# Products pre-added from five chunks to two instead of three, in a ring of four buffers

## The chip, the cores and the metric

The kernel runs on one core of one Trainium2 chip. The metric is the device time of one execution in microseconds (us); lower is better. Profiles come from the hardware profiler, one execution each.

## The reference

The input x has S = 2048 tokens of D = 640 numbers in bf16. It is layer-normalised, and the result xn feeds two branches whose outputs are added to x:

```python
xn = layernorm(x)                                  # no scale, no bias
# A: sliding, dilated attention; H = 32 heads of 20, W = 8 positions, step 2
q, k, v = split(xn @ wqkv)
logits[s, w] = (q[s] . k[s - 2*w]) * 20**-0.5      # -1e9 where s - 2*w < 0
o[s] = sum_w softmax(logits[s])[w] * v[s - 2*w]
A = o @ wo
# B: bilinear gated linear unit, F = 1536
B = ((xn @ w_gate) * (xn @ w_up)) @ w_down
out = x + A + B
```

## The kernel before

Everything stays in on-chip memory after loading. The 640 channels lie as NCH = 5 chunks of 128 partitions, tokens along the free dimension. The tokens are handled in two halves of HS = 1024 for the logits, in eight blocks of SB = 256 for the attention sums, in four blocks of 512 for gate and up, and in 16 tiles of 128 for the output.

*Stages on TensorE (PE).* Projections of q and k (L437, L444 for the first half, L424 for the second) and of v (L424); logits (L485); gate and up (`glu`, L577), each group five matmuls of 128x512; and the output tile (`tail`, L608): 12 matmuls with the weights WD of the down projection, then five with WO on the attention result VO. A tile takes two tails, one for each half of its 640 columns.

*Logits.* For each half there are four pairs of window positions (`pair`, `qk_steps`). VectorE (DVE) multiplies q by shifted k for both positions of a pair and all five chunks (L467). Instead of handing five chunks of products to PE it keeps the first NKC = 3 in a buffer SL, puts the other two in TMP, and adds these onto two of the kept ones (L475). PE then sums over channels with a matrix of ones, G: NKC chunks times four quarters of the tokens, 12 matmuls of 32 output rows a pair. The four quarters lie in four column groups of the array. Two pairs make one batch; `qk_logits` issues its 24 matmuls, and ScalarE (ACT) copies the result to LOG (L492).

*Softmax and attention.* `softmax_steps` has a head on DVE (maximum, L501; subtraction, L516), the exponential on ACT, and a rest on DVE (sums, reciprocal, product L525). `attn_move` copies the weights to the four channel rows of each head by 16 DMAs into ATB. `pv_steps(b)` makes the attention sum of block b: one product of 10240 elements into PVB (L551), then three adds (L546) of 5120, 2560 and 1280 elements, the last of which writes the block into VO. Tiles 2b and 2b + 1 read it in their WO matmuls.

*Other DVE work.* The multiplication of gate by up (L582), and the evacuation of each tail with the residual XR (L612).

*Memory.* SL is a ring of NSL = 3 buffers. WD and WO are later loaded to the same place, so `down_loads` and `out_loads` wait for the logits matmuls of the buffers that they overwrite. PVB lies on the last ring buffer and TMP.

*Order.* A Python planner writes the program out before it is built. It counts the estimated time of PE and DVE (`t_pe`, `t_dve`), walks through DVE's steps in a fixed order, and after each step lets `run_fill` issue PE work from a list up to DVE's time. A batch of logits gets a due time 0.3 us after its products, and is put into PE's order when `t_pe` has come to it. Down tails may be issued only when their block is:

```python
if it[0] == "dn":
    if pv_done[0] <= it[1] or not loaded:
        return
```

Gate and up for the token blocks 0 and 1 stand in the list ahead of the tails of block 0. Whatever a list item does on DVE (a multiplication, an evacuation) takes its place in DVE's order at the moment when the item is issued. Every engine then works in the order written, and semaphores hold back an instruction until what it needs is there.

Of the kernel before, what the change touches and what calls it, by code (L numbers as in the profile page):

```python
# [5 lines left out]
FP16 = mybir.dt.float16  # L6
ACT = mybir.ActivationFunctionType
ALU = mybir.AluOpType
# [3 lines left out]
NCH = 5  # L12
# [4 lines left out]
W = 8  # L17
# [11 lines left out]
HS = S // 2  # L29
SB = 256  # L30
# [11 lines left out]
class Sched:  # L42
# [50 lines left out]
    def op(self, eng, fn, r=(), w=(), dma=False, name="", group=None):  # L93
        X = _Op()
        X.eng, X.fn, X.name, X.dma = eng, fn, name, dma
        X.needs_tick, X.event, X.pre_know, X.idx = False, None, None, len(self.ops)
        rk = [k for a in r for k in self.keys(a)]
        wk = [k for a in w for k in self.keys(a)]
        deps = {}
        inorder = eng in ("pe", "act", "dve")  # L100
        for k in rk:
            st = self.state.get(k)
            if st is not None:
                for o in st[0]:
                    deps[o.idx] = o
        for k in wk:
            st = self.state.get(k)
            if st is None:
                continue
            if group is not None and st[2] == group and not st[1]:  # L110
                for o in st[3]:
                    deps[o.idx] = o
                continue
            for o in st[0]:
                if not (eng == "pe" and o.eng == "pe"):
                    deps[o.idx] = o
            for q in st[1]:
                if eng in ("pe", "act") and q.eng == eng and not q.dma:
                    continue
                deps[q.idx] = q  # L120
        last = {}
        keep = []
        for d in deps.values():
            if d.dma or d.eng == "pool":
                keep.append(d)
            else:
                b = last.get(d.eng)
                if b is None or b.idx < d.idx:
                    last[d.eng] = d
        X.deps = keep + list(last.values())  # L130
        for d in X.deps:
            if not d.dma:
                d.needs_tick = True
        for k in rk:
            st = self.state.get(k)
            if st is None:
                self.state[k] = [[], [X], None, []]
            elif inorder and st[1] and st[1][-1].eng == eng and not st[1][-1].dma:
                st[1][-1] = X
            else:  # L140
                st[1].append(X)
        for k in wk:
            st = self.state.get(k)
            if group is not None and st is not None and st[2] == group and not st[1]:
                st[0].append(X)
            else:
                before = [] if st is None else st[0] + st[1]
                self.state[k] = [[X], [], group, before]
        if dma:
            X.event = (self.nc.alloc_semaphore(f"dma{self.n_dma}"), 16)  # L150
            self.n_dma += 1
        self.ops.append(X)
        return X
# [59 lines left out]
def build_kernel(nc, A_x, A_wqkv, A_wo, B_x, B_w_gate, B_w_up, B_w_down, out):  # L213
    K = Sched(nc)
    op = K.op

    place = [16512]

    def sb(name, shape, dtype=BF16, at=None):
        n = mybir.dt.size(dtype)  # L220
        for s in shape[1:]:
            n *= s
        n = (n + 63) // 64 * 64
        if at is None:
            at = place[0]
            place[0] += n
        assert at + n <= 229344, (name, at + n)
        return K.sbuf(name, shape, dtype, at)
# [1 line left out]
    WG = sb("WG", [128, NCH, F])  # L230
    WU = sb("WU", [128, NCH, F])
    a_pr = place[0]
    NKC = 3
    NSL = 3
    WD = sb("WD", [128, NF, D], at=a_pr)
    WO = sb("WO", [128, NCH, D], at=a_pr + NF * D * 2)
    SL = [sb(f"SL{s}", [128, 2, NKC, HS], FP16) for s in range(NSL)]
    PVB = sb("PVB", [128, NCH, W, SB], FP16, at=place[0] - 2 * NKC * HS * 2)
    TMP = sb("TMP", [128, 2, NCH - NKC, HS], FP16)
    XNT = sb("XNT", [128, NCH, S])  # L240
    VO = sb("VO", [128, NCH, VP + S])
# [40 lines left out]
    def dma(o, i, r=(), w=(), name="", eng="sp", group=None):  # L282
# [8 lines left out]
       r=[IDENT[:]], w=[IDENT[:]], name="ident")  # L291
# [3 lines left out]
       r=[G[:]], w=[G[:]], name="g1")  # L295
    op("pool", lambda e: e.affine_select(G[:], G[:], pattern=[[-4, H]], compare_op=ALU.is_ge,
                                         fill=0.0, base=0, channel_multiplier=1),
       r=[G[:]], w=[G[:]], name="g2")
# [109 lines left out]
    def bank():  # L408
        b = bank_ring.pop(0)
        bank_ring.append(b)  # L410
        return b
# [46 lines left out]
    def qk_steps(h, p, s):  # L458
        kept, tmp = SL[s], TMP
        kp = KH[h][:, 0, 0:1].ap[0]  # L460

        def prod(o, c0, c1):
            q = QH[h][:, c0:c1, :]
            k = KH[h][:, c0:c1, 4 * p:4 * p + HS + 2]
            kw = bass.AP(k.tensor, k.offset, [kp, [2, 2], [KL, c1 - c0], [1, HS]])
            qw = q.unsqueeze(1).to_broadcast([128, 2, c1 - c0, HS])
            return lambda: op("dve", lambda e: e.tensor_tensor(o[:], qw, kw, ALU.mult), r=[q, k], w=[o[:]],  # L467
                              name=f"prod{h}_{p}_{c0}")

        a, b = kept[:, :, 0:NCH - NKC, :], tmp[:]  # L470
        return [
            (0.16 + 2 * NKC * HS / 1920, prod(kept, 0, NKC)),
            (0.16 + 2 * (NCH - NKC) * HS / 1920, prod(tmp, NKC, NCH)),
            (0.16 + 2 * (NCH - NKC) * HS / 1920,
             lambda: op("dve", lambda e: e.tensor_tensor(a, a, b, ALU.add), r=[a, b], w=[a], name=f"psum{h}_{p}")),  # L475
        ]

    def qk_logits(h, batch):
# [57 lines left out]
    def pv_steps(b):  # L536
# [8 lines left out]
        def add(o, x, y, name):  # L545
            return lambda: op("dve", lambda e: e.tensor_tensor(o, x, y, ALU.add), r=[x, y], w=[o], name=f"{name}_{b}")  # L546

        P4, P2 = PVB[:, :, 0:4], PVB[:, :, 0:2]
        return [
            (0.16 + NCH * W * SB / 1920,  # L550
             lambda: op("dve", lambda e: e.tensor_tensor(PVB[:], vw, aw, ALU.mult), r=[v, a], w=[PVB[:]], name=f"pv_{b}")),  # L551
            (0.16 + NCH * 4 * SB / 1920, add(P4, P4, PVB[:, :, 4:8], "pa4")),
            (0.16 + NCH * 2 * SB / 1920, add(P2, P2, PVB[:, :, 2:4], "pa2")),
            (0.16 + NCH * SB / 1920, add(o, PVB[:, :, 0], PVB[:, :, 1], "pa1")),
        ]
# [104 lines left out]
    for t0 in (0, 2):  # L660
# [3 lines left out]
        for which in (0, 1):  # L664
            for t in (t0, t0 + 1):
                b = bank()
# [16 lines left out]
    for t0 in (4, 6):  # L683
        for g in range(5):
            b = bank()
# [85 lines left out]
    def step(it):  # L771
        it[1]()
        t_dve[0] += it[0]
        run_fill(t_dve[0])

    slot = [0]

    def pair(h, p):
        s = slot[0] % NSL
        slot[0] += 1  # L780
        assert all(s != x for _, ps, _ in batches for _, x in ps)
        for it in qk_steps(h, p, s):
            step(it)
        return p, s
# [4 lines left out]
    def settle():  # L789
        while batches:  # L790
            run_fill(batches[0][2] + 0.01)
        t_dve[0] = max(t_dve[0], t_pe[0] + 1.6)

    batch(0, [pair(0, 0), pair(0, 1)])
    batch(0, [pair(0, 2), pair(0, 3)])
    headA, restA = softmax_steps(0)
    force_fill(QKB)
    t_dve[0] = max(t_dve[0], t_pe[0] + 0.8)
    b0 = pair(1, 0)
    settle()  # L800
    for it in headA:
# [34 lines left out]
def bass_parallel_sum__sliding_local_dilated__glu_gated_bilinear__prompt_kernel(  # L836
    nc, A_x, A_wqkv, A_wo, B_x, B_w_gate, B_w_up, B_w_down, out
):
    build_kernel(nc, A_x, A_wqkv, A_wo, B_x, B_w_gate, B_w_up, B_w_down, out)
# [28 lines left out]
```

## Time and profile before

| what | us |
|---|---|
| median of three runs | 262.35 (261.96 to 262.42) |
| the profiled execution | 262.42 |
| its span, first to last instruction | 260.7 |
| PE busy | 255.6 |
| DVE busy | 216.1 |
| ACT busy | 107.3 |

| DVE instruction | elements | count | ns each |
|---|---|---|---|
| L467 product into SL | 6144 | 8 | 3352 |
| L467 product into TMP | 4096 | 8 | 2302 |
| L475 add | 4096 | 8 | 2290 |
| L551 attention product | 10240 | 8 | 5488 |
| L546 attention adds | 5120, 2560, 1280 | 8 of each | 2817, 1484, 819 |
| L582 gate times up | 512 | 48 | 417 |
| L612 evacuation | 320 | 31 | 487 |

Successive instructions of an engine can overlap by some tens of ns, and a matmul's duration holds its way through the array, so start times tell more than durations where many follow each other. Idle time that is given with an arrow (`<-PE PS L608`) ended when that instruction did. In the chain, each piece is followed back to what released it.

### The profile page before, as it was taken

To read this page: it belongs to the slowest core of one execution; us is meant where nothing else is said; L and a number is where in the kernel's file an instruction comes from. 1 tells how busy PE (TensorE), PEld (TensorE's weight loads), DVE (VectorE), ACT (ScalarE), POOL (GpSimd) and SP (SyncE) were. 2 spreads that over 40 slices of the span, in tenths; PEclk is the share of its full clock that TensorE was granted. 3 is DMA by queue.
4 is the path that set the end of the run, shared out by engine and by line. 5 is a ranking of instruction groups with operands and counts; after the bars stand their busy time and mean duration, and the time that the engine had idled before them with its cause. 6 is when DMAs were issued, how large, how long until landed. Compare 5 with 4: busy or idle time off the path is not lost.

```text
span 260.7 us, 4018 instructions
## 1 busy us (share of the span) xinstructions
PE 255.6 (98%) x1669; PEld 150.7 (58%) x1669; DVE 216.1 (83%) x240; ACT 107.3 (41%) x193; POOL 6.7 (3%) x13
## 2 busy tenths in 40 slices
PE   7999999899999999999999999999999999999996
PEld 3899855354554444444467744446774444777775
DVE  5799889999999999998847999999999999422221
ACT  3565558555657555565630035551004555000000
POOL 2000050000200000000000000000000000000000
DMA  6968889400000275065001376000311000021301
GB/s 202 326 136 148 100 226 402 156 3 0 0 3 0 50 206 144 0 208 219 3 0 57 97 199 175 0 4 0 99 54 50 0 3 0 27 74 53 101 28 50
DMA packets 21922, 23.46 MB, mean 90 GB/s; under 512 B 9872, under 2 KB 19472, under 8 KB 21904
## 3 DMA queue, kind: packets, MB, share of 16 engines
q1 hardware_dynamic: 21760, 23.04, 31.2%
q8 instruction: 13, 0.21, 0.3%
q10 hardware_dynamic: 144, 0.16, 0.2%
q14 instruction: 5, 0.04, 0.0%
HBM read 14.42 MB, written 2.62 MB: 65 GB/s over the span
## 4 chain that ended last, share of the span: by engine, by line
PE 80%; DVE 14%; SPq 2%; DMA 2%; ACT 1%; issue 1%
PE PS L577 40%; PE PS L608 28%; PE PS L424 10%; DVE SL L467 3%; SPq L283 2%; DVE XNS L371 2%; PE PS L485 2%; DVE STATS L354 2%; DVE SL L475 2%; DVE TMP L467 2%; DVE STATS L348 2%; DMA XST<-in_A_x_dram 2%; DVE MV L360 1%; DVE SD L369 1%; ACT KH L451 0%
## 5 line engine op out<-in xcount | busy, mean ns | idle before, releaser
L577 PE MATMUL PS<-XNT,WG 128*128 128x512 bf16 x240 | 59.6, 379 | 0.0
L577 PE MATMUL PS<-XNT,WU 128*128 128x512 bf16 x240 | 59.6, 379 | 0.0
L608 PE MATMUL PS<-WD,HT 128*128 128x320 bf16 (+1 forms) x396 | 57.6, 295 | 0.0
L579 ACT ACTIVATE HT<-PS 128x512 bf16<-128x512 f32 x48 | 28.7, 598 | 58.2 <-PE PS L577 58.2
L608 PEld LDWEIGHTS PS<-WD,HT 128*128 128x128 bf16 x396 | 38.1, 98 | 14.7
L551 DVE TENSOR_TENSOR PVB<-VO,ATB 128x10240 f16<-128x10240 bf16 x8 | 43.9, 5488 | 0.1
L424 PE MATMUL PS<-XNT,WQKV 128*128 128x512 bf16 x200 | 43.9, 379 | 0.0
L612 DVE TENSOR_TENSOR FOUT<-PS,XR 128x320 bf16<-128x320 f32 (+1 forms) x33 | 15.5, 477 | 30.4 <-PE PS L608 30.1
L577 PEld LDWEIGHTS PS<-XNT,WU 128*128 128x128 bf16 x240 | 23.4, 98 | 28.5 <-issue 0.4
L577 PEld LDWEIGHTS PS<-XNT,WG 128*128 128x128 bf16 x240 | 23.4, 98 | 28.2 <-issue 0.4
L579 ACT ACTIVATE USX<-PS 128x512 bf16<-128x512 f32 x48 | 28.7, 597 | 22.2 <-PE PS L577 20.8
L424 PEld LDWEIGHTS PS<-XNT,WQKV 128*128 128x128 bf16 x200 | 23.3, 118 | 20.2 <-issue 0.8
L546 DVE TENSOR_TENSOR PVB<-PVB 128x5120 f16<-128x5120 f16 (+1 forms) x16 | 34.4, 2150 | 0.0
L467 DVE TENSOR_TENSOR SL<-QH,KH 128x6144 f16<-128x6144 bf16 x8 | 26.8, 3352 | 1.4 <-ACT KH L451 1.4
L608 PE MATMUL PS<-WO,VO 128*128 128x320 bf16 (+1 forms) x165 | 27.1, 295 | 0.0
L582 DVE TENSOR_TENSOR HT<-HT,USX 128x512 bf16<-128x512 bf16 x48 | 18.5, 417 | 4.2 <-ACT USX L579 4.2
L608 PEld LDWEIGHTS PS<-WO,VO 128*128 128x128 bf16 x165 | 15.9, 98 | 5.9
L475 DVE TENSOR_TENSOR SL<-SL,TMP 128x4096 f16<-128x4096 f16 x8 | 18.3, 2290 | 0.2
L467 DVE TENSOR_TENSOR TMP<-QH,KH 128x4096 f16<-128x4096 bf16 x8 | 18.4, 2302 | 0.0
L430 ACT ACTIVATE VO<-PS 128x512 bf16<-128x512 f32 x20 | 11.9, 597 | 9.8 <-PE PS L424 9.8
L437 PE MATMUL PS<-XNT,WQKV 128*128 128x128 bf16 x200 | 12.6, 220 | 0.2
L437 PEld LDWEIGHTS PS<-XNT,WQKV 128*128 128x128 bf16 x200 | 11.6, 118 | 1.2 <-DVE XNT L394 0.5
(49 smaller groups left out, 137.8 us busy)
## 6 DMA issues: line engine op xcount, KB each, us to landing
ATB<-LOG SPq DMA_DIRECT2D x32, 128.0 KB, 2.6
XR<-in_A_x_dram SPq DMA_DIRECT2D x16, 160.0 KB, 2.3
XST<-in_A_x_dram SPq DMA_DIRECT2D x15, 160.0 KB, 3.9
out_dram<-FOUT SPq DMA_DIRECT2D x15, 160.0 KB, 1.8
WG<-in_B_w_gate_dram SPq DMA_DIRECT2D x1, 1920.0 KB, 9.5
WU<-in_B_w_up_dram SPq DMA_DIRECT2D x1, 1920.0 KB, 13.8
WD<-in_B_w_down_dram SPq DMA_DIRECT2D x1, 1920.0 KB, 8.2
WQKV<-in_A_wqkv_dram SPq DMA_DIRECT2D x10, 160.0 KB, 3.8
```

Source lines behind the costliest of these rows:

```text
L424: op("pe", (lambda l, x, c: lambda e: e.matmul(PS[:, b, :], l, x, start=(c == 0), stop=(c == NCH - 1)))(l, x, c), r=[l, x], w=[PS[:, b, :] ...
L430: op("act", lambda e: e.activation(o, PS[:, b, :], ACT.Copy), r=[PS[:, b, :]], w=[o], name=f"pev{which}_{m}_{j}")
L437: op("pe", (lambda o, l, x, st, sp: lambda e: e.matmul(o, l, x, start=st, stop=sp))(o, l, x, st, sp), r=[l, x], w=[o], name=f"pp{which}_{m ...
L467: return lambda: op("dve", lambda e: e.tensor_tensor(o[:], qw, kw, ALU.mult), r=[q, k], w=[o[:]], name=f"prod{h}_{p}_{c0}")
L475: lambda: op("dve", lambda e: e.tensor_tensor(a, a, b, ALU.add), r=[a, b], w=[a], name=f"psum{h}_{p}")),
L546: return lambda: op("dve", lambda e: e.tensor_tensor(o, x, y, ALU.add), r=[x, y], w=[o], name=f"{name}_{b}")
L551: lambda: op("dve", lambda e: e.tensor_tensor(PVB[:], vw, aw, ALU.mult), r=[v, a], w=[PVB[:]], name=f"pv_{b}")),
L577: op("pe", (lambda l, x, c: lambda e: e.matmul(PS[:, b, :], l, x, start=(c == 0), stop=(c == NCH - 1)))(l, x, c), r=[l, x], w=[PS[:, b, :] ...
L579: op("act", lambda e: e.activation(o, PS[:, b, :], ACT.Copy), r=[PS[:, b, :]], w=[o], name=f"guev{which}_{m}_{j}")
L582: h_pending.append(lambda: op("dve", lambda e: e.tensor_tensor(h, h, o, ALU.mult), r=[h, o], w=[h], name=f"h{m}_{j}"))
L608: op("pe", (lambda l, x, i, b: lambda e: e.matmul(PS[:, b, 0:wid], l, x, start=(i == 0), stop=(i == n - 1)))(l, x, i, b), r=[l, x], w=[PS[ ...
L612: op("dve", (lambda o, xr, b: lambda e: e.tensor_tensor(o, PS[:, b, 0:wid], xr, ALU.add))(o, xr, b), r=[PS[:, b, :], xr], w=[o], name=f"fi ...
```

## The change

Two chunks of products are kept instead of three. The three others go to TMP; two of them are added onto the two kept ones, and then the last is added onto the first kept one. So there are two adds for each pair in place of one, and eight logits matmuls in place of twelve. SL becomes a ring of four smaller buffers, which is entered at the last one, and PVB is put on the last ring buffer and the larger TMP as before. The total memory is the same.

```diff
-    NKC = 3
-    NSL = 3
+    NKC = 2
+    NSL = 4
...
-    PVB = sb("PVB", [128, NCH, W, SB], FP16, at=place[0] - 2 * NKC * HS * 2)
+    PVB = sb("PVB", [128, NCH, W, SB], FP16, at=place[0] + 4 * (NCH - NKC) * HS - 2 * NCH * W * SB)
...
-        a, b = kept[:, :, 0:NCH - NKC, :], tmp[:]
+        def add(a, b):
+            return lambda: op("dve", lambda e: e.tensor_tensor(a, a, b, ALU.add), r=[a, b], w=[a], name=f"psum{h}_{p}")
+
         return [
             (0.16 + 2 * NKC * HS / 1920, prod(kept, 0, NKC)),
             (0.16 + 2 * (NCH - NKC) * HS / 1920, prod(tmp, NKC, NCH)),
-            (0.16 + 2 * (NCH - NKC) * HS / 1920,
-             lambda: op("dve", lambda e: e.tensor_tensor(a, a, b, ALU.add), r=[a, b], w=[a], name=f"psum{h}_{p}")),
+            (0.16 + 4 * HS / 1920, add(kept[:, :, 0:2, :], tmp[:, :, 0:2, :])),
+            (0.16 + 2 * HS / 1920, add(kept[:, :, 0, :], tmp[:, :, 2, :])),
         ]
...
-        s = slot[0] % NSL
+        s = (slot[0] + NSL - 1) % NSL
```

The numbers ahead of the steps are the planner's times for them in us; with them, and with the shorter batches (0.2175 us for each pair and chunk), the planner writes another order. From L467 on, the line numbers of the changed kernel are up to two higher.

## The prediction

> **What bounds the kernel now.** I read the page first, for which engine is never idle.
>
> ```profile
> PE 255.6 (98%) x1669; PEld 150.7 (58%) x1669; DVE 216.1 (83%) x240; ACT 107.3 (41%) x193; POOL 6.7 (3%) x13
> PE   7999999899999999999999999999999999999996
> DVE  5799889999999999998847999999999999422221
> PE 80%; DVE 14%; SPq 2%; DMA 2%; ACT 1%; issue 1%
> ```
>
> TensorE (PE) is busy throughout and carries 80% of the chain of waits. But VectorE (DVE) is just as full, at 9 tenths, up to five sixths of the span: its 83% is an average over a full part and an empty end. A change that sends work from PE to DVE sends it to an engine with almost no room before 222 us. So I read the chain in order of time next, for where PE last waited for DVE.
>
> ```profile
> 49.35 0.83 PE PS L485 x12
> 50.18 14.16 PE PS L424 x65
> 64.34 1.44 PE PS L485 x24
> ...
> 110.59 1.41 PE PS L485 x24
> 112.00 20.61 PE PS L577 x95
> 132.61 18.47 PE PS L608 x136
> ```
>
> L485 are the logits matmuls (two pairs to a batch), L577 gate and up, L608 the output tiles ("tails"). From 50 us PE never stops. Note the 20.6 us of gate/up work between the last logits batch and the first tail. The third view is DVE's timeline under the first tails.
>
> ```profile
> 122.92 5.48 DVE L551 TENSOR_TENSOR PVB<-VO,ATB 128x10240 f16<-128x10240 bf16 x1
> ...
> 139.98 1.48 DVE L546 TENSOR_TENSOR PVB<-PVB 128x2560 f16<-128x2560 f16 x1
> 141.88 0.49 DVE L612 TENSOR_TENSOR FOUT<-PS,XR 128x320 bf16<-128x320 f32 x1 [0.42 <-PE PS L608]
> 142.29 0.81 DVE L546 TENSOR_TENSOR VO<-PVB 128x1280 bf16<-128x1280 f16 x1
> ```
>
> The L546 add at 142.29 completes attention block 1 at 143.10. The tail of token tile 2 needs it after four tails and its own 12 WD matmuls: 132.61 + 4 x 2.31 + 1.63 = 143.48. The margin is 0.4 us, and it exists because the big product of block 1 (L551, 122.92) ran before the tails began. The bracket shows the danger: DVE works in program order, and an evacuation (L612) makes it stand until PE has finished that tail.
>
> **PE saves 1.9 us.** Per pair 12 logits matmuls become 8, 32 fewer in all. A batch of 24 took 1.41 us, 0.0588 each: 32 x 0.0588 = 1.88 us.
>
> **DVE pays 10 us.** The two products keep their sizes, 6144 and 4096 elements, in the other order, and the 4096 add stays; a 2048 add comes on top, which reads what the 4096 add wrote. L546 gives its price: 2.82 us for 5120 elements and 1.48 for 2560 are 0.52 ns an element and 0.15 fixed, so 1.22 us, of which 0.08 overlap the next start; waiting for its predecessor costs 0.11 more. That is 1.25 us a pair, 10.0 in all, and a pair goes from 7.81 to 9.06. The first four pairs (33.56 us on) run back to back.
>
> Batch 1 now sits behind 95 L424 matmuls instead of 80. PE reaches it at 47.61 + 3.24 = 50.85, waits for the second pair (33.56 + 18.12 + 0.1 = 51.8) and leaves at 52.3. Batch 2 comes 75 matmuls later, 68.6; its second pair ends at 69.9, so PE waits 0.9 and leaves at 70.45. At the same amount of work the old kernel stood at 71.2: 0.7 gained. Batches 3 and 4: on DVE follow pair 5 (69.8 to 78.9), the maximum and subtraction (72.69 to 75.34 before, 2.65), pair 6 with six gate/up multiplications at 0.34 (between the adds they also hide the 0.11 and 0.11 of waiting: 8.84 + 2.04, to 92.4), the sum and division (83.47 to 88.19 before, 4.7, to 97.1), pairs 7 and 8 with five and six multiplications (10.5 and 10.9, to 118.5). PE adds up to 70.45 + 6.6 (30 L424) + 19.4 (90 L577) = 96.5 for batch 3, then 0.94 and 26.0 to 123.4 for batch 4: DVE is 4 and 5 us ahead, no wait, another 0.94 saved. PE is then ready for the first tail at 130.94 instead of 132.61. The ring of four and the moved slots add no wait here: each slot's last reader is a batch or more back.
>
> **What the slower pairs move: two things on the path.** The schedule is written from estimated times, so a later DVE puts logits batches later in PE's order. Comparing the two programs' instruction orders, only 30 gate/up matmuls (6.5 us) stand between batch 4 and the first tail, where 95 (20.6 us) stood.
>
> First, WD and WO are loaded into the slots that batch 4 reads. The SP queue issued WD 1.3 us into batch 4, landing took 8.2 us, WO's 9.7. Now WD goes out near 123.75 and lands at 131.95, WO goes out at 124.2 and lands at 133.9. The first tail wants WO at 130.94 + 1.63 = 132.57, so it waits 1.35 us, where before there were ten to spare. Nothing else stands before these two on SP: the attention copies and XR loads end near 109. With WG's 9.5 us as the price this wait is 1.3 longer; with all loaded in time it is gone.
>
> Second, and larger: DVE now begins block 0's attention at 118.5 (5.4 + 2.74 + 1.48 + 0.82 and three multiplications: it ends at 130, in time for 132.57), and the whole first half of the next softmax (L501, L516) and block 1 follow *behind* the first four evacuations. In DVE's new order stand: evacuation, evacuation, maximum, evacuation, maximum, evacuation, maximum, subtraction, L551, three L546. With the first tail ended at 134.6 by WO, the fourth ends at 141.5. Then: evacuation 0.41, maximum 0.32, subtraction 1.15, product 5.51, adds 2.85 + 1.51 + 0.82 = 12.6 us, block 1 at 154.1. PE wants it at 141.5 + 1.63 = 143.2. All of PE's queue stands behind that matmul: 11.0 us without work. Before, only 0.41 + 0.81 stood between the fourth tail and this point.
>
> After it, DVE catches up. Tails 4 to 7 need block 3; its adds lie between evacuations as block 1's did before, with the same margin (0.41 + 0.82 against 1.63). The later blocks end over ten us ahead of their tails. Evacuations stay inside the ring of eight banks, and the attention products of the last blocks, which now run beside the last tails, hold evacuations back by at most 5.4 us against a ring of 18. So nothing is given back and nothing more lost: 11.0 + 1.35 - 1.67 = +10.7 us.
>
> **PE's rate after the gap.** No gap in this trace is this long. The nearest row is the start of the kernel:
>
> ```profile
> 1.88 1.06 PE L402 MATMUL PS<-ZERO 128*128 128x512 bf16 x2
> 2.31 1.06 PE L402 MATMUL PS<-ZERO 128*128 128x512 bf16 x2
> ```
> ```profile
> 3.88 0.82 PE L402 MATMUL PS<-ZERO 128*128 128x512 bf16 x3
> 4.31 0.38 PE L402 MATMUL PS<-ZERO 128*128 128x512 bf16 x1
> ```
>
> Successive answers start 0.43 us apart for one matmul, later 0.43 for two: PE begins at half its rate. Ten matmuls start within 3.25 us where nine intervals at 0.216 take 1.94, a loss of 1.3 us. The granted clock reads 1.00 there too, so I go by the spacing. After the 0.9 us gap at 48.4 the second 12 logits matmuls took 0.83 us like the first: no loss. Eleven us are nearer to the start, so I take 1.3, with 0 as the low end and, if half the rate lasts twice as long, 2.6 as the high one.
>
> The Trainium skill ("TensorE: Matmul & The Clock Gate", Part 1, "What's actually happening") has a rule that speaks against this change: an idle window of about 3.4 us halves PE's clock, and about 3.4 us of sustained work restore it. By it an estimate of the loss is half of 3.4, or 1.7 us, and the sum would end 0.4 later than by the row.
>
> **Sum.** 10.7 + 1.3 = +12.0. The profiled execution took 262.42 us for a span of 260.7, and is 0.07 above the median: 262.42 + 12.0 - 0.07 = 274.3 us.
>
> **Rivals.**
>
> *Faster.* The gap does not open, and the PE saving survives: 262.35 - 1.67 = 260.7 us. That takes block 1 finished before 143.2, hence its product started by 132.6, before the first evacuation. The PE saving and the PE-bound chain speak for it; DVE's new order, with the product behind the fourth evacuation, against. 4%.
>
> *The added DVE work costs double*, as the new 2048 add reads one strided chunk, a form no row shows. At twice 1.22 us each pair takes 1.2 more, batch 1 then waits 2.4 longer and batch 2 again 2.4; batches 3 and 4 have 4 to 5 us of room and the big gap stays: 274.3 + 4.8 = 279.1. 6%.
>
> *Block 3 misses its tail as well.* If its product is held up by a multiplication it waits for, the second group of tails waits too, by up to a product's 5.5 us: 274.3 + 5.5 = 279.8. The margin is 0.4 us by my walk, as block 1's was before, where PE did not wait. 7%.
>
> *The change does not do what it says*: if batches of 16 still take 1.4 us, the saving goes: 276.2. 3%.
>
> **How the numbers follow.** My forecast, one gap of about 11 us at the third token tile, has 80%: 274.3. Its range: without the slow restart 273.0, without the WO wait 271.6; with restart at 2.6 and WD at WG's price 276.9, and half a us for the walk, 277.4. This holds most of the 80% and the smaller forms of the rivals, so 271.6 to 277.4. About 0.2% (0.5 us) can be told from no change. Slower 0.95, within 0.01, faster 0.04.
>
> **What would show it.** In the new trace: L485's successor with 64 matmuls and batches near 0.94 us; a new DVE add group of eight at 1.22 us; a wait of PE (or its weight load) of about 11 us for the L546 add into VO at 143 us; a first tail of about 3.7 us, held by WO; tail matmuls after the gap spaced 0.27 instead of 0.136 us for some 2.5 us; no second gap; the last tails 289 matmuls in 37 us. If PE's busy share stays at 98%, or the gap is at another tile, I am wrong.

## The result, and the profile after

The changed kernel takes 274.97 us (median of four runs, 274.71 to 275.08) against 262.35: a ratio of 1.048, with a 95% interval of 1.0465 to 1.0501 (the brackets behind later ratios are such intervals too). The profiled execution took 275.08 us for a span of 273.2, 12.7 above the profiled execution before. The prediction was 274.3, in a range of 271.6 to 277.4.

First the page, with the busy tenths of PE and DVE, the granted clock and the chain by engine:

```profile
PE   7999999999999999999790499999999999999996
DVE  5899799999999999999159519996799999997222
PEclk9999999999999999999998599999999999999999
PE 66%; DVE 25%; DMA 5%; SPq 2%; issue 1%; ACT 1%; DVEq 0%
```

PE now has a hole, the 0 between 143 and 150 us. DVE has two dips of its own just ahead of it (the 1 and the 5): it, too, stood idle before PE did. The clock row, which the page before did not have, falls in the hole and is lowest in the next slice, in which PE starts again. On the chain DVE and DMA have gained what PE lost, 14% of the span. The chain in order of time names the places (start, us, what):

```profile
122.54 1.00 PE PS L487 x16
...
123.57 9.68 DMA WO<-in_A_wo_dram
133.25 0.14 issue
133.38 7.78 PE PS L610 x56
...
141.19 0.49 DVE FOUT L614
...
143.05 5.50 DVE PVB L553
...
152.96 0.84 DVE VO L548
153.79 0.05 issue
153.84 9.77 PE PS L610 x56
```

From the last logits batch the chain goes through WO's landing to the tails, through the fourth tail's evacuation (L614) into DVE, there through the product and the adds of block 1, and back to PE at 153.84. The first line's batch of 16 took 1.00 us where 24 took 1.41. The waits put numbers on the two links (us in total, times, longest):

```profile
PE PS L610 <- DVE VO L548: 11.1, 1, 11.1
PE PS L610 <- DMA WD<-in_B_w_down_dram: 1.3, 1, 1.3
```

The second line is WD alone; WO held the tail a little longer. The first tail could have begun near 130.1 us and wanted WO at 131.7; it got it at 133.38, 1.7 us late. Last, stretches of time with the busy time of each engine, then the granted clock and the share of DMA:

```profile
143.00:153.00 10.00, 0.00 (x0) 0.00 (x0) 9.90 (x5) 1.91 (x1) 0.00 (x0) 0.73 0.07 18
153.00:158.00 5.00, 4.16 (x16) 2.40 (x17) 1.27 (x2) 0.00 (x0) 0.00 (x0) 0.51 0.00 0
158.00:163.00 5.00, 5.00 (x39) 3.61 (x37) 0.98 (x2) 0.00 (x0) 0.00 (x0) 1.00 0.24 70
```

In the first, DVE is full and PE empty. In the second PE has work again for 4.16 us, at 0.51 of its clock: 16 matmuls, where the next five us hold 39.

### The profile page after: what moved, and what is told of

Same layout as the page of the kernel before. It is cut to its first block, busy times and chain, and to the rows that moved or that the text cites. A ratio compares the mean times of both kernels' runs of the same rounds, so it can differ in the third digit from the quotient of the medians.

```text
span 273.2 us, 3962 instructions
## 1 busy us (share of the span) xinstructions
PE 256.4 (94%) x1637; PEld 150.7 (55%) x1637; DVE 225.8 (83%) x248; ACT 107.7 (39%) x193; POOL 4.2 (2%) x13
## 4 chain that ended last, share of the span: by engine, by line
PE 66%; DVE 25%; DMA 5%; SPq 2%; issue 1%; ACT 1%; DVEq 0%
PE PS L579 36%; PE PS L610 27%; DVE SL L471 5%; DVE TMP L467 5%; DMA WO<-in_A_wo_dram 4%; DVE SL L467 3%; PE PS L424 2%; SPq L283 2%; DVE PVB L553 2%; DVE XNS L371 2%; DVE STATS L354 2%; DVE STATS L348 2%; DVE PVB L548 2%; DMA XST<-in_A_x_dram 1%; PE PS L487 1%
## 5 line engine op out<-in xcount | busy, mean ns | idle before, releaser
L610 PE MATMUL PS<-WD,HT 128*128 128x320 bf16 (+1 forms) x396 | 58.9, 300 | 1.3 <-DMA WD<-in_B_w_down_dram 1.3
L610 PEld LDWEIGHTS PS<-WD,HT 128*128 128x128 bf16 x396 | 38.7, 99 | 17.2 <-ACT USX L581 1.8
L614 DVE TENSOR_TENSOR FOUT<-PS,XR 128x320 bf16<-128x320 f32 (+1 forms) x33 | 15.5, 479 | 35.0 <-PE PS L610 34.9
L610 PE MATMUL PS<-WO,VO 128*128 128x320 bf16 (+1 forms) x165 | 27.8, 300 | 11.2 <-DVE VO L548 11.1
L548 DVE TENSOR_TENSOR PVB<-PVB 128x5120 f16<-128x5120 f16 (+1 forms) x16 | 34.4, 2151 | 0.1
L471 DVE TENSOR_TENSOR SL<-SL,TMP 128x4096 f16<-128x4096 f16 (+1 forms) x16 | 28.1, 1756 | 0.3
L467 DVE TENSOR_TENSOR TMP<-QH,KH 128x6144 f16<-128x6144 bf16 x8 | 26.9, 3367 | 0.0
L467 DVE TENSOR_TENSOR SL<-QH,KH 128x4096 f16<-128x4096 bf16 x8 | 18.3, 2285 | 0.9 <-ACT KH L451 0.9
L437 PE MATMUL PS<-XNT,WQKV 128*128 128x128 bf16 x200 | 12.5, 220 | 0.2
```

The lines of the kernel that those rows point to most:

```text
L437: op("pe", (lambda o, l, x, st, sp: lambda e: e.matmul(o, l, x, start=st, stop=sp))(o, l, x, st, sp), r=[l, x], w=[o], name=f"pp{which}_{m ...
L471: return lambda: op("dve", lambda e: e.tensor_tensor(a, a, b, ALU.add), r=[a, b], w=[a], name=f"psum{h}_{p}")
L610: op("pe", (lambda l, x, i, b: lambda e: e.matmul(PS[:, b, 0:wid], l, x, start=(i == 0), stop=(i == n - 1)))(l, x, i, b), r=[l, x], w=[PS[ ...
L614: op("dve", (lambda o, xr, b: lambda e: e.tensor_tensor(o, PS[:, b, 0:wid], xr, ALU.add))(o, xr, b), r=[PS[:, b, :], xr], w=[o], name=f"fi ...
```

## The experiments

The theory is that of the prediction: the added DVE time, *through the planner's order*, puts block 1 behind the fourth evacuation and batch 4 close to the tails. The main rival is plainer: DVE has 10 us more to do and is the bound in any order.

### Evacuations behind block 1

```diff
-                if pv_done[0] <= it[1] or not loaded:
+                if pv_done[0] <= (it[1] | 1) or not loaded:
```

> The changed kernel, with one line of the planner different: a tail may be issued only when both attention blocks of its group of four token tiles have been written out, so that the evacuations follow block 1 on DVE. Same instructions, other DVE order. Theory (the order of DVE makes the gap): block 1 ends near 142.1 us, PE wants it at 142.6, so the 11.06 us wait and the 2.0 us of half-rate matmuls behind it go; the wait for WO (1.9 us) stays: 275.0 - 13.1 = 261.9 us, 261.5 to 263. Rival (the 10 us of added DVE work is the bound in any order): block 1 or a later one is late by 5 us and more: 267 us or above.

Measured: 261.97 us, a ratio to the kernel before of 0.9989 (0.998 to 0.9999). PE's timeline at the third token tile, then DVE's:

```profile
141.34 1.79 PE L610 MATMUL PS<-WD,HT 128*128 128x320 bf16 x12
142.97 0.84 PE L610 MATMUL PS<-WO,VO 128*128 128x320 bf16 x5
```
```profile
141.71 0.83 DVE L548 TENSOR_TENSOR VO<-PVB 128x1280 bf16<-128x1280 f16 x1
```

Block 1 ends at 142.54, the matmul that needs it starts at 142.97 without idle time. The same instructions on the same data are 13.0 us faster in another order. The rival falls: DVE's 10 us alone make no gap. The wait for WO is still there.

### Work for PE in the gap

```diff
+                if i == NF and (t, nb) == (2, 0):
+                    z = ZERO[:, 0:1].to_broadcast([128, JB])
+                    for _ in range(48):
+                        op("pe", lambda e: e.matmul(PS[:, 7, :], ZERO[:], z, start=True, stop=True), ...)
```

> The changed kernel with 48 matmuls on zeros (128x512, 10.4 us at 0.216 each) put on PE ahead of the matmul that waits for block 1, into a bank that nobody reads then. They fit into the 11.06 us gap. Theory (the slow 22 matmuls after the gap come from the clock that fell in it): the 2.0 us go, 273.0 us, and the granted clock stays at 1.00. Rival (they are slow for another cause, such as weights or DVE's evacuations): 275.0 us, spacing still 0.27 us.

Measured: 272.81 us, 2.2 less than the changed kernel. The stretches again:

```profile
143.00:153.00 10.00, 10.00 (x47) 4.30 (x45) 9.90 (x4) 1.91 (x1) 0.00 (x0) 1.00 0.06 16
153.00:158.00 5.00, 4.39 (x33) 3.13 (x33) 1.62 (x3) 0.00 (x0) 0.00 (x0) 1.00 0.01 3
```

The clock stays at 1.00, and the 56 matmuls of the remaining tails take 7.78 us on the chain instead of 9.77:

```profile
153.69 7.78 PE PS L615 x56
```

The 2.0 us are the clock's, and not DVE's or the weights': those are unchanged here.

### The old order with the new products

The planner is given the old times (the added add costs it nothing, the batches count as long as before); the instructions are the changed kernel's.

```diff
-            (0.16 + 2 * NKC * HS / 1920, prod(kept, 0, NKC)),
-            (0.16 + 2 * (NCH - NKC) * HS / 1920, prod(tmp, NKC, NCH)),
+            (0.16 + 2 * 3 * HS / 1920, prod(kept, 0, NKC)),
+            (0.16 + 2 * 2 * HS / 1920, prod(tmp, NKC, NCH)),
...
-            (0.16 + 2 * HS / 1920, add(kept[:, :, 0, :], tmp[:, :, 2, :])),
+            (0.0, add(kept[:, :, 0, :], tmp[:, :, 2, :])),
...
-        t_pe[0] = max(t_pe[0], at) + 0.44 + 0.2175 * NKC * len(batch)
+        t_pe[0] = max(t_pe[0], at) + 0.44 + 0.2175 * 3 * len(batch)
```

> The changed kernel, but the planner is given the old times (the second add at 0, batches as long as before), so every batch of logits and every tail stands where it stood in the kernel before, with 95 gate/up matmuls behind batch 4. Theory (order decides, DVE's added work costs only where PE meets it): PE waits at batches 1 and 2, some 2.7 and 3 us instead of 1.0 and 0, and about 1 us at batch 4; WO is early and block 1 in time: about 266 us, 264 to 268. Rival (DVE's total is the bound): block 1 late as well, 271 us or more. Rival (only the planner's order costs, DVE's work is free): 260.7 us.

Measured: 266.85 us, a ratio of 1.0176 (1.0161 to 1.0191). No wait for block 1 and none for WO is left; PE waits for the adds (L471) at three batches, 5.3 us in all. PE's timeline:

```profile
47.38 0.62 PE L487 MATMUL PS<-SL,G 128*32 128x512 f16 x8
51.31 0.61 PE L487 MATMUL PS<-SL,G 128*32 128x512 f16 x8 [3.32 <-DVE SL L471]
51.86 15.91 PE L424 MATMUL PS<-XNT,WQKV 128*128 128x512 bf16 x65
67.70 0.61 PE L487 MATMUL PS<-SL,G 128*32 128x512 f16 x8
69.42 0.62 PE L487 MATMUL PS<-SL,G 128*32 128x512 f16 x8 [1.10 <-DVE SL L471]
```

The total is as expected, its parts are not quite. The first wait is 3.3 us, and the 65 matmuls after it take 15.8 from start to start where they took 14.16 before: the clock fell here too. What PE lost there it did not have to wait at batch 2, where 1.1 came instead of 3.

So the planner's new order is not foolish where it stands: without it DVE's time shows at the batches. It saves nearly all of those 5 us of waits (0.4 is left) and the fall of the clock with them, and loses 13 us at the third token tile.

### The added step alone

The kernel before, with an add of 2048 elements on TMP that nobody reads, told to the planner. Nothing is saved on PE, and the ring, the buffers and the batches are the old ones.

```diff
+            (0.16 + 2 * HS / 1920,
+             lambda: op("dve", lambda e: e.tensor_tensor(x0, x0, x1, ALU.add), r=[x0, x1], w=[x0], name=f"extra{h}_{p}")),
```

> The kernel before (three chunks, ring of three, 12 logits matmuls a pair) with one more add of 2048 elements per pair on DVE, on TMP after its last use, and its time told to the planner. Nothing is saved on PE. Theory (the added DVE step, through the planner's order, makes the gap): batch 4 again goes late, 40 gate/up matmuls before the first tail, block 1's product behind the fourth evacuation; the subtraction stands one evacuation earlier, so the gap is about 9.5 us, plus 2.0 us of half-rate matmuls, WO nearly in time: 274 us, 273 to 276. Rival (the gap comes from the ring, the buffers' places or the shorter batches): 262.4 to 263.5 us.

Measured: 273.53 us, a ratio of 1.0433 (1.0418 to 1.0449), with one wait of PE for block 1 of 9.6 us:

```profile
152.54 1.51 PE L611 MATMUL PS<-WO,VO 128*128 128x320 bf16 x5 [9.60 <-DVE VO L549]
```

The added DVE step by itself gives the gap; it needs neither the ring, nor the slots, nor the shorter batches. The gap is 1.5 us shorter than in the changed kernel, as expected, because the subtraction stands ahead of the fourth evacuation here.

### Without the wait for WO

The first experiment's kernel, and one line ahead of the first softmax:

```diff
     settle()
+    t_dve[0] -= 4.0
     for it in headA:
```

> The first experiment's kernel (tails gated by both blocks), and batches 3 and 4 of the logits put some 4 us earlier into PE's order (the planner's DVE time is set back by 4 us ahead of the softmax of the first half), so that 50 gate/up matmuls, 10.8 us, stand between batch 4 and the first tail. Theory: WD and WO land before they are wanted and the 1.7 us of waiting for them go; but then PE wants block 1 at 141.3 us and DVE, which did not move, ends it at 142.2: about 0.9 us of it come back as a wait for block 1: 261.2 us. Rival (the WO wait is all that is left): 260.3 us. Rival (earlier batches meet DVE): PE waits at batch 3 or 4, 262 us or above.

Measured: 261.73 us, a ratio of 0.9983 (0.9974 to 0.9993). WD was issued at 118.84 instead of 123.48, and the first tail ran through from 129.96. But at the third tile:

```profile
139.20 1.79 PE L610 MATMUL PS<-WD,HT 128*128 128x320 bf16 x12
142.21 0.85 PE L610 MATMUL PS<-WO,VO 128*128 128x320 bf16 x5 [1.22 <-DVE VO L548]
```

Most of what WO gave was taken back by block 1, 1.2 us of it (0.9 was expected). The two waits lay behind each other on one path: taking the first away uncovers the second.

### Block 1 first

The same, with the second softmax's head moved behind block 1 on DVE:

```diff
     pv(0)
     settle()
-    for it in headB:
-        step(it)
     bank_ring[:] = bank_ring + [6, 7]
     pv(1)
+    for it in headB:
+        step(it)
```

> The same, and the attention of block 1 ahead of the second softmax's head on DVE, so that block 1 ends about 2.65 us earlier, near 139.5 us, before PE wants it at 141.3. Theory: nothing of the gap, the slow restart or the WO wait is left, and what remains of the change is its saving on PE, 1.9 us less the waits at batches 1 and 2: 260.3 us, 1.5 to 2 us below the kernel before. Rival (DVE's added 10 us are paid somewhere else, at a later block or at evacuations): 261.5 us or above.

Measured: 260.12 us, a ratio to the kernel before of 0.9921 (0.9908 to 0.9935). DVE's timeline, then PE's:

```profile
138.89 0.82 DVE L548 TENSOR_TENSOR VO<-PVB 128x1280 bf16<-128x1280 f16 x1
```
```profile
141.04 0.84 PE L610 MATMUL PS<-WO,VO 128*128 128x320 bf16 x5
```

Block 1 is ready 1.3 us early. This kernel beats both, by 2.0 and 14.9 us, with all the added DVE work in it. Behind batch 2 no wait of PE for DVE is left on the chain.

### The control

The kernel before with two of the edits above:

```diff
-                if pv_done[0] <= it[1] or not loaded:
+                if pv_done[0] <= (it[1] | 1) or not loaded:
...
-    for it in headB:
-        step(it)
     bank_ring[:] = bank_ring + [6, 7]
     pv(1)
+    for it in headB:
+        step(it)
```

> A control: the kernel before (three chunks kept) with the two edits to DVE's order, the gate of the tails and block 1 ahead of the softmax's head. Theory: it had no gap and no WO wait to lose, so nothing changes: 262.2 us, within 0.4. Rival (the new order is better in itself, and the gain of the kernel with all edits is not the change's): near 260.5 us.

Measured: 262.18 us, a ratio of 1.0002 (0.9993 to 1.0011). The two edits of DVE's order do nothing for the old products, so the 2.0 us of the kernel above are the change's, with an order that lets them through. Two things make them up: the shorter batches (1.7 us in all), and the wait of 0.9 us at batch 1 that the kernel before has and the kernel above has not, less the 0.5 that it waits at batch 2. The third edit, the earlier batches, was not tried with the old products; their WO was never late.

## Why the prediction was right

*PE saves 1.9 us*: a batch went from 1.41 to 0.98 to 1.01 us, near 0.42 each, so 1.7 in all. A third fewer matmuls took less than a third off a batch.

*DVE pays 1.25 us a pair*: the pairs start 9.05 us apart (41.62, 50.67), as worked out, and the new add takes 1223 ns, as the line through two other adds said. The rival in which this form costs double is refuted.

*Batches 1 and 2*: here the walk was off. DVE's first product started at 32.51 and not at 33.56. It reads only two chunks now and waits for two of K's evacuations instead of three (0.5 us), which I had overlooked; the rest was an earlier start of this execution. PE then did not stand at batch 1 and stood 0.4 at batch 2, not 0.5 and 0.9.

*WD and WO*: issued at 123.13 and 123.57, landing after the same 8.2 and 9.7 us. WO's wait was 1.7 us where 1.35 was predicted, since PE came earlier and WO by less.

*The gap*: 11.06 us of PE against 11.0, at the predicted tile, for the predicted L548, with the predicted steps between the fourth evacuation (141.19) and block 1's end (153.78): 12.6. The experiments show the cause, and no second gap came: block 3's margin held.

*The slow restart*: 2.0 us against 1.3, inside its bounds. The row used, the start of the kernel, had matmuls at half rate for some 2.5 us; after the gap it was 4.1 (153.84 to 157.9). The Trainium skill's rule ("TensorE: Matmul & The Clock Gate", Part 1, "What's actually happening") was the better guide here: by its 3.4 us of work the loss is estimated at 1.7; measured were 2.0.

*The sum*: the place and the cause of the loss were foreseen; that the number came so close is partly luck. The profiled spans differ by 12.5 us, and the sum said 12.0. PE was ready for the first tail 2.5 us ahead of the kernel before (130.1 against 132.61) and not 1.67, because it waited less at batches 1 and 2. That 0.8 hides more than half of what was too small elsewhere: the restart by 0.7, and the two stops by 0.7 together (they delayed PE by 1.8 and 11.2 us, counted from the starts of its matmuls, where 1.35 and 11.0 stood). The upper end of the range had a slip that cost nothing: with WD landing after 9.5 us and WO as before, the prediction's own times give a wait of 2.3 us, 1.0 more than 1.35 and not 1.3.

## What to carry to other kernels

Before work is moved from a full engine to one that has slack by the span, look at the slack of the stage, and at what the slower engine's time moves in a schedule that is written out from it: the 10 us of added work cost PE half a us of waiting (at batch 2) once they lay in the right order, and 13 us in the order that the planner chose. On an engine that works in program order, an evacuation that waits for PE must not stand ahead of work that PE's next tiles wait for. Where a wait goes, say what comes next on the path; taking away the first of two waits in a row gave back only their difference here.

## What was not expected of the hardware

The clock fell late, and after a short gap too. In the changed kernel PE's last matmul ended at 142.8 us and the granted clock went to 0.50 at 147.7:

```profile
147.50:147.70 0.20, 0.00 (x0) 0.00 (x0) 0.20 (x1) 0.00 (x0) 0.00 (x0) 1.00 0.00 0
147.70:147.90 0.20, 0.00 (x0) 0.00 (x0) 0.20 (x1) 0.00 (x0) 0.00 (x0) 0.50 0.00 0
```

In the old order with new products, a gap of only 3.3 us (48.0 to 51.3) had its fall when PE was already back at work; the stretches:

```profile
51.50:52.50 1.00, 1.00 (x11) 0.39 (x4) 1.00 (x1) 0.52 (x1) 0.00 (x0) 1.00 0.00 0
52.50:53.50 1.00, 1.00 (x4) 0.39 (x3) 1.00 (x2) 0.08 (x1) 0.00 (x0) 0.51 0.00 0
```

The matmuls ran at full rate for a us and then at half, and lost 1.7 us (15.84 against 14.16), nearly as much as after the gap of 11. What counted was not the gap's length but how long PE worked at half rate: 3.4 us here (the clock was back at 1.00 from 55.9), 4.1 there. This gap cost half as much again as it measures. The gap of 0.9 us in the kernel before and the one of 1.2 us in the kernel without the wait for WO brought no fall: the granted clock of both executions is 1.00 on average. Why the fall comes so late no run here shows.
